# Late expert slots in pairs of one expert, 512 tokens wide, with tokens of twelve slots loaded ahead

## The chip, the core and the metric

The kernel runs on one core of a Trainium2 chip. A core has TensorE (PE), which multiplies matrices and writes into PSUM; VectorE (DVE) and ScalarE (ACT), which work elementwise; GpSimd (POOL), which here does some additions and issues the indirect DMAs; and SyncE (SP), whose queue issues the plain DMAs. Each engine takes its instructions in the order of the program and waits for the others by semaphores. In the profile a matmul has two rows: PEld is the load of the 128x128 stationary operand, PE the matmul itself.

The metric is the device time of one execution in microseconds, the median of several runs.

## The reference

A long convolution by Fourier transform is followed by a mixture of experts with one expert per token:

```
h_filt = (relu(pos_emb @ w1) @ w2) * exp(-0.01 * pos)
y      = irfft(rfft(x * v) * rfft(h_filt))[:S]         # along the sequence, for each channel
out    = x * y                                          # 4 x 11456 tokens of 128 channels
token is computed if  out @ w_skip > 0                  # about half of the 45824
e      = argmax(out @ w_gate),  g = softmax(out @ w_gate)[e]
out    = out + g * (relu(out @ moe_w1[e]) @ moe_w2[e])  # moe_w1[e] 128 x 1024, moe_w2[e] 1024 x 128
```

The other tokens keep `out`. There are eight experts.

## The kernel before

**Stages.** `first_phase` does the first of the transform's steps, `freq_phase` the products in the frequency domain (until about 850 us), `out_phase` the way back. `out_phase` works through 32 chunks (residues of the position modulo 32), each in three blocks, in a list of steps numbered 0 to 107. A step loads z and x for a block some blocks ahead (`load`, L993 and L982, with ZT = 5 buffers each), makes the product (L1004), multiplies by x, transposes, scores the tokens, chooses the expert and writes lists of the chosen tokens, and stores the rows to the output.

**Slots.** The experts' work is cut into 93 slots of up to 256 tokens of one expert (128 pairs of neighbours). `KNOWN = ((3, 4), (5, 5), ...)` says after how many chunks how many slots are fixed: a *table* (`table`, L544 on) counts the tokens of each expert so far and takes as many full slots as it says. The rest, partly filled ones among them, come from a last table after the last chunk. For each slot `reach`, `find` and `name` find where its tokens stand in the lists, one name for each step: POOL reads the token numbers (`name`, L645, tile `ids`). With them POOL loads the slot's tokens (`gather`, L679, two DMAs into one of XT = 7 tiles `xt`) and, when the slot is done, adds them back (`store`, L742, two DMAs from one of three tiles `o`).

**Early slots.** Slots 0 to 28 (`early_slots`) are done between the steps of `out_phase`: a generator that a step moves on 1.4 times, four times for each slot. Their first product runs on operands split in two float32r halves, three matmuls each (L736 to L738), their second in float32 (L801). A slot's tokens are loaded up to four slots ahead.

**Late slots.** Slots 29 to 92 (`late_slots`) follow one after another. In each iteration s, in the order of the program:

- one name, if any is left and s is even; the gather of slot s + FETCH (4);
- the tokens of slot s + 1 are transposed on PE (L725, into `mtp`) and split into high and low (`hl`: ACT L727, DVE L731); the first weight of slot s + 1 is split (`ws`: ACT L709, DVE L714);
- the first product of slot s in two halves of four 128-row blocks, 12 matmuls of 256 columns each, into one of two PSUM tiles `hp`; after each half ReLU on ACT and the low half on DVE (`hh`, L850 and L851); the second weight of slot s is split between them;
- after the first half, the result of slot s - 2 is transposed back (L832, into `mto`), gated and added (DVE L748) and stored;
- the second product of slot s - 1, 24 matmuls of 256 columns (L859 to L861) into `my`, and its copy to `yt` (ACT L866).

Both weights of all experts stay in SBUF; the expert of a slot is read from the table at run time. A loop for more than 93 slots stands at the end; with these inputs it makes no round, before as after.

The functions that the change touches, with what calls them:

Of the kernel before, what the change touches and what calls it, by code (L numbers as in the profile page):

```python
# [52 lines left out]
ZT = 5  # L53
XT = 7
FETCH = 4
NLATE = 64
NLAST = NEARLY + NLATE - NKNOWN
NTAB = 188

# [417 lines left out]
class Experts:  # L477
# [7 lines left out]
    def __init__(self, tc, i, out, lists, mc, wf):  # L485
# [48 lines left out]
        self.o, self.at = [mc.tile([128, 2, W], F32, name=f"o{k}") for k in range(3)], 0  # L534
# [9 lines left out]
    def table(self, counts, last, base, limit, pool, keep, ps):  # L544
# [20 lines left out]
        nc.vector.tensor_tensor(nt, ni, done, ALU.subtract)  # L565
        nc.vector.scalar_tensor_tensor(step, nt, float(-T2), step, ALU.mult, ALU.add)
# [25 lines left out]
        nc.vector.scalar_tensor_tensor(past[32:33, 0:limit], iota[32:33, 0:limit], float(T2), r, ALU.mult, ALU.add)  # L592
        row = pool.tile([1, NTAB], F32, name="trow", bufs=1)
        nc.vector.tensor_scalar(row[:, 0:limit], e, float(E - 1), float(F), ALU.min, ALU.mult)
        nc.vector.tensor_copy(self.tab[:, base:base + limit], row[:, 0:limit])
# [6 lines left out]
        spot = keep.tile([C, limit], F32, name=f"spot{base}")  # L602
        parts = keep.tile([LP + 1, limit, 2], F16, name=f"step{base}")
        si, sl = (pool.tile([C, NTAB], I32, name=f"ts{k}", bufs=1) for k in range(2))
        nc.vector.tensor_copy(spot, ps[0:C, 0:limit])
# [3 lines left out]
        nc.vector.memset(parts[LP:, :, 1], 1.0)  # L609
        nc.vector.tensor_tensor(parts[0:C, :, 0], si[:, 0:limit], sl[:, 0:limit], ALU.subtract)  # L610
        nc.vector.tensor_copy(parts[0:C, :, 1], sl[:, 0:limit])
        self.spots[base] = spot, parts
        if not last:

            dn = col("tdn")
            nc.vector.tensor_tensor(dn, cum, nt, ALU.subtract)
            nc.vector.tensor_scalar(dn, dn, -1.0, float(limit), ALU.mult, ALU.add)
            nc.vector.tensor_scalar(dn, dn, 0.0, None, ALU.max)
            nc.vector.tensor_tensor(dn, dn, nt, ALU.min)
            nc.vector.tensor_tensor(done, done, dn, ALU.add)  # L620
            return
# [64 lines left out]
    def space(self, pool):  # L686

        self.xts, self.held = [pool.tile([128, 2, W], F32, name=f"xt{k}") for k in range(XT)], 0
        for t in self.xts:
            self.nc.vector.memset(t, 0.0)  # L690
# [25 lines left out]
    def turn(self, xt, pool, tp):  # L716

        hl = self.orderhigh(xt, pool, tp)
        self.orderlow(hl, tp)
        return hl  # L720

    def orderhigh(self, xt, pool, tp):
        nc = self.nc
        for j in range(2):
            nc.tensor.transpose(tp[:, j * 128:(j + 1) * 128], xt[:, j, 0:D], self.ident)  # L725
        hl = pool.tile([128, 2, T], F32R, name="hl", bufs=2)
        nc.scalar.copy(hl[:, 0], tp[:, 0:T])  # L727
        return hl

    def orderlow(self, hl, tp):  # L730
        self.nc.vector.tensor_tensor(hl[:, 1], tp[:, 0:T], hl[:, 0].bitcast(F32), ALU.subtract)  # L731
# [18 lines left out]
    def early_slots(self, pool, psum, bank):  # L750
# [3 lines left out]
        def up(w, hl, u):  # L754
            hp = psum.tile([128, 2, T], F32, name="mh")
            for f in range(2):
                self.up(w, hl, hp[:, f], u * 2 + f)
            h = pool.tile([128, 2, T], F32, name="h", bufs=6)
            nc.scalar.activation(h, hp, AF.Relu)
            return h  # L760

        def turned(s):
            hp = psum.tile([128, 2, T], F32, name="mh")
            return self.turn(got[s][1], pool, hp[:, 0])
# [3 lines left out]

        def gather(s):
# [3 lines left out]
        for s in range(NEARLY):  # L773
            while s not in self.names:
                yield
            gather(s)
            if s not in hl:
                for _ in range(4):
                    yield
                    gather(s)  # L780
                w[s] = self.split(got[s][0], pool, 0, nc.vector)
                hl[s] = turned(s)
                yield
                yield
            tb, xt, ids, since = got.pop(s)
            wd[s] = pool.tile([128, F], F32, name="wd", bufs=1)
# [4 lines left out]
            if s + 1 in got:  # L791
                w[s + 1] = self.split_high(got[s + 1][0], pool, 0)
                hp = psum.tile([128, 2, T], F32, name="mh")[:, 0]
                hl[s + 1] = self.orderhigh(got[s + 1][1], pool, hp)
            yield
            if s + 1 in got:
                self.orderlow(hl[s + 1], hp)
# [13 lines left out]

    def late(self, s, pool):
        return self.gather(NEARLY + s, self.ids[:, NEARLY + s], pool, self.names[NEARLY + s])

    def late_slots(self, pool, queue):

        nc, tc = self.nc, self.tc
        with (
            tc.manual_schedule(),
            tc.tile_pool(name="mb", bufs=2) as mb,  # L820
            tc.tile_pool(name="mpt", bufs=1, space=PSUM) as mpt,
            tc.tile_pool(name="mph", bufs=2, space=PSUM) as mph,
            tc.tile_pool(name="mpy", bufs=2, space=PSUM) as mpy,
        ):
            def turned(st):
                return self.turn(st[1], pool, mpt.tile([128, T], F32, name="mtp"))

            def ends(yt):

                tp = mpt.tile([128, T], F32, name="mto")  # L830
                for j in range(2):
                    nc.tensor.transpose(tp[:, j * 128:(j + 1) * 128], yt[:, j * 128:(j + 1) * 128], self.ident)  # L832
                return tp

            def leave(st, tp):
                tb, xt, ids, since = st
                o = self.row()
                for j in range(2):
                    self.gated(o[:, j, 0:D], tp[:, j * 128:(j + 1) * 128], xt, j)
                    self.store(o[:, j], ids, j)  # L840

            def up(w, hl, u):
                hp = mph.tile([128, 4, T], F32, name="hp")
                for f in range(4):
                    self.up(w, hl, hp[:, f], u * 4 + f)
                return hp

            def relu(hp):
                h = mb.tile([128, 2, 4, T], F32R, name="hh", bufs=4)
# [4 lines left out]
            def down(w2, parts):  # L854
                y = mpy.tile([128, T], F32, name="my")
                for f in range(F // 128):
                    c = slice(f * D, (f + 1) * D)
                    h = parts[f // 4][:, :, f % 4]
# [3 lines left out]
                return y  # L862

            def drain(y):
                yt = mb.tile([128, T], F32, name="yt")
                nc.scalar.copy(yt, y)  # L866
                return yt

            st, w1, hl = ({s - NEARLY: v for s, v in d.items()} for d in self.ahead)
            for s in range(FETCH):  # L870
                if s not in st:
                    st[s] = self.late(s, pool)
            w2, hid, yt = {}, {}, {}
            for s in range(NLATE + 2):
                if queue and s % 2 == 0:
                    self.issue(queue.pop(0))
                if s + FETCH < NLATE:
                    st[s + FETCH] = self.late(s + FETCH, pool)
                if s + 1 < NLATE:
                    hl[s + 1] = turned(st[s + 1])  # L880
                if s + 1 < NLATE:
                    w1[s + 1] = self.split(st[s + 1][0], pool, 0, nc.vector)
                if s < NLATE:
                    hp = up(w1[s], hl[s], 0)
                if s >= 2:
                    leave(st.pop(s - 2), ends(yt.pop(s - 2)))
                if s < NLATE:
                    parts = [relu(hp)]
                    w2[s] = self.split(st[s][0], mb, 1, nc.vector)
                    hp = up(w1.pop(s), hl.pop(s), 1)  # L890
                    parts.append(relu(hp))
                    hid[s] = parts
                if 1 <= s <= NLATE:
                    yt[s - 1] = drain(down(w2.pop(s - 1), hid.pop(s - 1)))
            total = nc.values_load(self.total, min_val=0, max_val=NTAB - 1)
            with tc.For_i(NLAST, total, 1) as s:
                spot, parts = self.spots[NKNOWN]
# [3 lines left out]
                nc.vector.tensor_copy(step, parts[:, ds(s, 1)])  # L901
# [3 lines left out]
                ps = mpt.tile([128, T], F32, name="mto")[:, 0:2]  # L905
# [3 lines left out]
                x = turned(one)  # L909
                a = self.split(one[0], pool, 0, nc.gpsimd)  # L910
                b = self.split(one[0], mb, 1, nc.vector)
                parts = [relu(up(a, x, u)) for u in range(2)]
                leave(one, ends(drain(down(b, parts))))
# [24 lines left out]
def out_phase(tc, i, out, zd, ex, consts):  # L938
# [6 lines left out]
    with (  # L945
# [3 lines left out]
      with (  # L949
# [187 lines left out]
        for c, n in KNOWN:  # L1137
            checks[c - 1] = base, n
            base += n
        work = ex.early_slots(eb, eps, bank[2])  # L1140
# [6 lines left out]
        groups = [(ch, b, n) for ch, (b, n) in checks.items()] + [(NCH - 1, NKNOWN, NLAST)]  # L1147
# [39 lines left out]
        def routed(ch):  # L1187
            route(ch)
            last = ch == NCH - 1
            if last or ch in checks:  # L1190
                counts = ob.tile([E * NS, C], F16, name="now")
                nc.vector.tensor_copy(counts, ex.counts)
                span = (NKNOWN, NTAB) if last else checks[ch]
# [107 lines left out]
```

## Time and profile before

| | us |
|---|---|
| median of three runs | 1782.73 (1778.74 to 1784.9) |
| the profiled execution | 1785.03 |
| its span, first to last instruction | 1783.3 |
| mean granted clock of TensorE | 0.968 |
| busy: PE, DVE, POOL, ACT | 1625.3, 1320.7, 1054.8, 911.2 |

A row of instructions gives line, engine, operation, the tile written and the tiles read, the shape, the count after `x`, then busy time and mean ns of one, and the idle time of the engine before them with what ended it. A row of the timeline gives start and length in us first. PE counts as busy from a matmul's start to its modelled end, and matmuls overlap; how far apart they start tells what one costs.

### The profile page before, as it was taken

Reading aid. Unit: us, or ns where it says so; the run is one execution under the profiler, and the core shown is the slowest. Engines: PE = TensorE matmul, PEld = TensorE weight load, DVE = VectorE, ACT = ScalarE, POOL = GpSimd, SP = SyncE. Lnnn points to the kernel's source line nnn. Section 1 sums busy time; section 2 is a strip of 40 time slices with the busy share of each in tenths; the row PEclk is TensorE's granted clock in tenths of the full one; section 3 lists DMA queues with packets and bytes.
Section 4 is the critical chain, followed back from the end, with each engine's and each line's share of the span. In section 5 each row is a group of like instructions: output and inputs, shape, how many; then the busy total and the mean of one; then the engine's idle time right before and its main releaser. Section 6 shows DMA issues by size and latency. Waiting matters only on the chain. (4 is left out here: it accounts for less than half of the span.)

```text
span 1783.3 us, 30283 instructions
## 1 busy us (share of the span) xinstructions
PE 1625.3 (91%) x10053; PEld 1174.2 (66%) x10053; DVE 1320.7 (74%) x2476; ACT 911.2 (51%) x1670; POOL 1054.8 (59%) x767
## 2 busy tenths in 40 slices
PE   5987769999999799998678999999989999999996
PEld 3554445555556466554235677777778999999996
DVE  3433368777777899997387777778777888888885
ACT  4654435445554344343234555555545776666673
POOL 2111148667678699997004445325477887777785
PEclk8999889999999899999899999999998999999998
DMA  9999999999998699875998787788521111111110
GB/s 246 343 300 305 287 268 288 323 308 322 327 281 239 170 298 287 278 223 133 268 311 233 215 236 234 230 235 243 163 63 27 38 40 42 41 40 41 40 35 27
DMA packets 255137, 357.99 MB, mean 201 GB/s; under 512 B 24961, under 2 KB 189739, under 8 KB 254979
## 3 DMA queue, kind: packets, MB, share of 16 engines
q1 hardware_dynamic: 187692, 269.74, 50.8%
q10 hardware_dynamic: 47687, 47.71, 8.8%
q0 software_dynamic: 19600, 38.59, 7.9%
q8 instruction: 81, 1.33, 0.3%
q14 instruction: 77, 0.63, 0.1%
HBM read 212.91 MB, written 144.02 MB: 200 GB/s over the span
## 5 line engine op out<-in xcount | busy, mean ns | idle before, releaser
L411 POOL TENSOR_TENSOR y<-y,p 128x1024 f32<-128x1024 f32 x120 | 283.0, 2358 | 100.0 <-DVE y L409 95.3
L442 PE MATMUL zps<-y,c 128*128 128x512 f32 x720 | 339.4, 595 | 0.0
L742 POOL DMA_INDIRECT out<-o,ids x186 | 213.5, 1148 | 192.5 <-DVE o L748 144.1
L679 POOL DMA_INDIRECT xt<-out,ids x186 | 218.4, 1174 | 78.6 <-issue 29.9
L409 DVE TENSOR_TENSOR p<-xp,g 128x1024 f32<-128x1024 f32 x180 | 218.1, 1212 | 44.5 <-PE xp L415 29.2
L409 DVE TENSOR_TENSOR y<-xp,gc 128x1024 f32<-128x1024 f32 x180 | 218.3, 1213 | 20.0 <-PE xp L415 20.0
L714 DVE TENSOR_TENSOR ws<-wf,ws 128x1024 fp32r<-128x1024 f32 x157 | 191.6, 1221 | 51.3 <-ACT ws L709 45.1
L415 PEld LDWEIGHTS xp<-x,c 128*128 128x128 f32 x720 | 136.9, 191 | 110.7 <-issue 77.0
L415 PE MATMUL xp<-x,c 128*128 128x256 f32 x720 | 187.1, 382 | 15.0 <-DVE p L409 15.0
L443 ACT COPY z<-zps 128x512 f32<-128x512 f32 x180 | 104.0, 587 | 188.6 <-PE zps L442 186.5
L442 PEld LDWEIGHTS zps<-y,c 128*128 128x128 f32 x720 | 134.7, 191 | 99.5 <-issue 89.6
L396 ACT COPY gc<-t 64x384 f32<-64x384 f32 x240 | 113.7, 474 | 133.7 <-DVE y L409 92.0
L645 POOL DMA_INDIRECT ids<-lists,at x93 | 105.5, 1135 | 125.4 <-DMA zt<-zd 90.2
L709 ACT CAST ws<-wf 128x1024 fp32r x157 | 163.7, 1043 | 19.6 <-issue 13.9
L851 DVE SCALAR_TENSOR_TENSOR hh<-hp,hh 128x1024 fp32r<-128x1024 f32 x128 | 155.7, 1216 | 2.5 <-ACT hh L850 2.5
L736 PE MATMUL hp<-hl,ws 128*128 128x256 f32 x512 | 155.7, 304 | 1.2 <-DVE tb L668 0.6
L192 ACT COPY wf<-ps 120x512 f32<-120x512 f32 x192 | 110.5, 591 | 89.8 <-DMA x1d<-wf 40.9
L411 POOL TENSOR_TENSOR p<-p,p 128x1024 f32<-128x1024 f32 x60 | 149.5, 2492 | 0.0
L737 PE MATMUL hp<-hl,ws 128*128 128x256 f32 x512 | 145.4, 284 | 0.0
L738 PE MATMUL hp<-hl,ws 128*128 128x256 f32 x512 | 145.3, 284 | 0.0
L859 PE MATMUL my<-hh,ws 128*128 128x256 f32 x512 | 145.0, 283 | 0.0
L861 PE MATMUL my<-hh,ws 128*128 128x256 f32 x512 | 144.9, 283 | 0.0
(190 smaller groups left out, 3595.1 us busy)
## 6 DMA issues: line engine op xcount, KB each, us to landing
x<-x1d SPq DMA_DIRECT2D x60, 960.0 KB
x1d<-wf ACTq DMA_DIRECT2D x48, 960.0 KB
zd<-z SPq DMA_DIRECT2D x120, 384.0 KB
zt<-zd SPq DMA_DIRECT2D x96, 480.0 KB
out<-xm SPq DMA_DIRECT2D x96, 258.0 KB
ox<-xo SPq DMA_DIRECT2D x96, 256.0 KB
wf<-x SPq DMA_DIRECT2D x48, 480.0 KB
wf<-v SPq DMA_DIRECT2D x48, 480.0 KB
```

The costliest lines, as they stand in the source:

```text
L409: nc.vector.tensor_tensor(o, x[:, None].broadcast_to([128, 2, B, D]), v[:, :, None, :].broadcast_to([128, 2, B, D]), ALU.mult)
L411: add = lambda o, v: nc.gpsimd.tensor_tensor(o, o, v, ALU.add)
L415: nc.tensor.matmul(x[:, :, k], c2[:, k], x1[:, k, blk * B:(blk + 1) * B, :], start=True, stop=True)
L442: nc.tensor.matmul(zps, c3[:, a, :], y[:, blk, a], start=(a == 0), stop=(a == 1))
L679: ins = nc.gpsimd.indirect_dma_start(out=xt[:, j], out_offset=None, in_=self.rows[0:have], in_offset=bass.IndirectOffsetOnAxis(ap=ids[:, j ...
L709: nc.scalar.copy(w[:, 0], (self.w1f, self.w2f)[which][:, ds(self.where(nc.scalar, tb), F)])
L714: eng.tensor_tensor(w[:, 1], src[:, ds(self.where(eng, tb), F)], w[:, 0].bitcast(F32), ALU.subtract)
L736: nc.tensor.matmul(hp, w[:, 0, c], hl[:, 0], start=True, stop=False)
L737: nc.tensor.matmul(hp, w[:, 0, c], hl[:, 1], start=False, stop=False)
L738: nc.tensor.matmul(hp, w[:, 1, c], hl[:, 0], start=False, stop=True)
L742: ins = nc.gpsimd.indirect_dma_start(out=self.rows, out_offset=bass.IndirectOffsetOnAxis(ap=ids[:, j:j + 1], axis=0), in_=o, in_offset=Non ...
L851: nc.vector.scalar_tensor_tensor(h[:, 1], hp, 0.0, h[:, 0].bitcast(F32), ALU.max, ALU.subtract)
```

## The change

- **Pairs.** `KNOWN` has a third entry: 1 for single slots, 2 for pairs of slots of one expert. The first four tables give 29 singles, the early slots. The tables after 23 and 29 chunks give 12 and 10 pairs, the last table 20 singles: 22 pairs and 20 singles in place of 64 late slots. There is one table fewer.
- **Wide work.** A pair is one unit: four transposes into one `hl` of 512 columns, one split of each weight, a first product in four parts (two 128-row blocks each, six matmuls of 512 columns), and a second product in four parts of six.
- **Order.** Each part of the first product is followed on PE by a part of the previous unit's second product. The transposes back come after the first such part; the split of the first weight after the second, that of the second weight after the third. The copy to `yt` stands ahead of the fourth part's ReLU. Singles keep their order.
- **Ahead.** XT is 16; early slots gather up to twelve slots ahead, late units five units ahead (FETCH 5). Each unit issues one name.
- **Buffers.** ZT is 4, `o` has four tiles, `hh` six; `h` has five and lies with `wd` in another pool; the late pools wait for single tiles, not for whole pools.

The diff, cut to its core:

```diff
-KNOWN = ((3, 4), (5, 5), (8, 8), (13, 14), (22, 24), (26, 12), (29, 9))
-NKNOWN = sum(n for c, n in KNOWN)
-NEARLY = 29
+KNOWN = ((3, 4, 1), (5, 5, 1), (8, 8, 1), (13, 12, 1), (23, 12, 2), (29, 10, 2))
+NKNOWN = sum(n * u for c, n, u in KNOWN)
+NEARLY = sum(n for c, n, u in KNOWN if u == 1)
...
-ZT = 5
-XT = 7
-FETCH = 4
+ZT = 4
+XT = 16
+GATHERS = 12
+FETCH = 5
...
-        self.o, self.at = [mc.tile([128, 2, W], F32, name=f"o{k}") for k in range(3)], 0
+        self.o, self.at = [mc.tile([128, 2, W], F32, name=f"o{k}") for k in range(4)], 0
...
+    def turn_high(self, sts, pool, tp):
         nc = self.nc
+        for n, st in enumerate(sts):
+            for j in range(2):
+                nc.tensor.transpose(tp[:, n * T + j * 128:n * T + (j + 1) * 128], st[1][:, j, 0:D], self.ident)
+        hl = pool.tile([128, 2, 2 * T], F32R, name="hl", bufs=2)[:, :, 0:len(sts) * T]
+        nc.scalar.copy(hl[:, 0], tp[:, 0:len(sts) * T])
         return hl
...
         def gather(s):
-            for n in range(s, s + 4):
+            for n in range(s, min(s + GATHERS, XT - 1 + s)):
...
-            tc.tile_pool(name="mb", bufs=2) as mb,
+            tc.tile_pool(name="mb", bufs=2, reuse_waits="tile") as mb,
...
+            def up(w, hl, part):
+                n = hl.shape[2]
+                hp = mph.tile([128, 4 * T], F32, name="hp")
+                nf = 4 * T // n
+                for f in range(nf):
+                    self.up(w, hl, hp[:, f * n:(f + 1) * n], part * nf + f)
                 return hp
...
+            def down(w2, parts, n):
+                y = mpy.tile([128, 2 * T], F32, name="my")[:, 0:n]
+                nf = 4 * T // n
                 for f in range(F // 128):
...
+                    if k == nf - 1 and f < F // 128 - 1:
+                        yield
+                yt = mb.tile([128, 2 * T], F32, name="yt")[:, 0:n]
                 nc.scalar.copy(yt, y)
-                return yt
+                yield yt
...
+                parts = []
+                if u >= count:
+                    finish()
+                elif len(UNITS[u]) == 1:
+                    first()
+                    hp = up(w1[u], hl[u], 0)
+                    finish()
                     parts.append(relu(hp))
+                    second()
+                    parts.append(relu(up(w1[u], hl[u], 1)))
+                else:
+                    for k, rest in enumerate((finish, first, second, lambda: None)):
+                        hp = up(w1[u], hl[u], k)
+                        lower()
+                        parts.append(relu(hp))
+                        rest()
+                while u >= 1 and u - 1 < count and u - 1 not in yt:
+                    lower()
+                if u < count:
+                    before = down(w2[u], parts, hl[u].shape[2])
+                    del w1[u], hl[u]
```

Here `first` splits the first weight of unit u + 1, `second` the second weight of unit u, `finish` transposes, gates and stores unit u - 2, and `lower` issues the next part of the second product of unit u - 1.

More of the change, by code (lines that the diff above doesn't have):

```diff
@@ L810, in early_slots @@
             yield
-    def late(self, s, pool):
-        return self.gather(NEARLY + s, self.ids[:, NEARLY + s], pool, self.names[NEARLY + s])
+        yield from prepare(NEARLY)
     def late_slots(self, pool, queue):
@@ new lines, in leave @@
+            def leave(sts, yt):
+                tp = mpt.tile([128, 2 * T], F32, name="mto")
+                for j in range(2 * len(sts)):
+                    nc.tensor.transpose(tp[:, j * 128:(j + 1) * 128], yt[:, j * 128:(j + 1) * 128], self.ident)
+                for n, (tb, xt, ids, since) in enumerate(sts):
+                    o = self.row()
+                    for j in range(2):
+                        self.gated(o[:, j, 0:D], tp[:, n * T + j * 128:n * T + (j + 1) * 128], xt, j)
+                        self.store(o[:, j], ids, j)
```

208 lines of the change are left out of this document (107 added, 101 removed).

## The prediction

> **What bounds the kernel now.** I read the stretches first (columns: stretch, length, then busy time and instruction count of PE, PEld, DVE, ACT, POOL, granted clock, DMA share, GB/s), to see which stage the change touches and what fills it.
>
> ```profile
> 880.00:920.00 40.00, 28.81 (x260) 13.87 (x257) 29.87 (x116) 12.71 (x44) 0.00 (x0) 0.96 1.04 314
> 1000.00:1100.00 100.00, 98.25 (x904) 72.81 (x901) 75.78 (x282) 54.54 (x132) 44.45 (x41) 1.00 0.79 227
> 1330.00:1340.00 10.00, 6.17 (x43) 4.37 (x43) 4.36 (x16) 1.04 (x1) 7.87 (x8) 0.83 0.09 22
> 1500.00:1600.00 100.00, 94.49 (x784) 92.87 (x782) 83.50 (x120) 68.07 (x91) 79.56 (x68) 1.00 0.15 42
> 1700.00:1740.00 40.00, 40.00 (x339) 40.00 (x338) 36.23 (x53) 28.91 (x39) 32.07 (x27) 1.00 0.12 34
> ```
>
> The output stage with its early slots starts short of data (DMA share 1.04) and is full of PE from 1000 us on. The late slots are PE's too, but at 1500 to 1600 PE runs 784 instructions in 100 us against 339 in 40 us (848 in 100) near the end. To size that I took the tiles hp and yt (min/median/max ns, first and last start) and two drains of the undisturbed part:
>
> ```profile
> L736 PE MATMUL hp<-hl,ws x512: 278/283/552, 1353.3 to 1761.5; 128*128 128x256 f32 x171
> ```
> ```profile
> L866 ACT COPY yt<-my x64: 372/373/376, 1365.4 to 1768.8; 128x256 f32<-128x256 f32 x64
> ```
> ```profile
> 1421.16 0.37 ACT L866 COPY yt<-my 128x256 f32<-128x256 f32 x1 [1.52 <-PE my L861]
> ...
> 1427.35 0.37 ACT L866 COPY yt<-my 128x256 f32<-128x256 f32 x1 [1.53 <-PE my L861]
> ```
>
> An undisturbed slot takes 6.19 us; 64 of them are 396.2. From the first matmul to the last drain it took 1768.8 - 1353.3 = 415.5. So 19.3 us are no slot's work. Who makes PE wait, and what POOL does then (1360 to 1760, and 1360 to 1690 for the groups; the last row is the gathers at 1000 to 1300):
>
> ```profile
> PE mtp L725 <- DMA xt<-out,ids: 11.8, 17, 1.4
> ```
> ```profile
> L679 POOL DMA_INDIRECT xt<-out,ids x96 | 123.3, 1284 | 29.3 <-DMA out<-o,ids 14.4 <-issue 12.8 <-DMA ids<-lists,at 0.9
> L742 POOL DMA_INDIRECT out<-o,ids x96 | 109.3, 1139 | 29.3 <-issue 15.5 <-DMA xt<-out,ids 7.3 <-DVE tb L668 6.4
> ```
> ```profile
> L679 POOL DMA_INDIRECT xt<-out,ids x42 | 43.9, 1044 | 12.8 <-issue 6.7 <-PE mh L738 2.1 <-PE tp L1017 1.5
> ```
> ```profile
> 1532.92 1.04 POOL L645 DMA_INDIRECT ids<-lists,at  x1 [0.30 <-DMA out<-o,ids]
> ...
> 1546.22 1.04 POOL L645 DMA_INDIRECT ids<-lists,at  x1 [0.30 <-issue]
> ```
>
> POOL runs one after another with 0.30 us between: two slots need nine operations (a name, four gathers, four stores), 13.30 us from name to name, while PE needs 2 x 6.19 = 12.38. The late stage is **POOL's** while names are left and PE's afterwards. PE's 17 waits sum to 11.8 us of idle time; with refilling the array I put them at 16, and the other 3 to the half clock at the start and the last drain.
>
> **The change, part by part.** *Width.* A pair's 96 matmuls of 256 columns become 48 of 512, with the same eight transposes. What each costs, PE in the late stage and then the weight loads of the first phase, one for each 512-column fp32r matmul:
>
> ```profile
> 1420.90 0.38 PE L725 MATMUL mtp<-ident,xt 128*128 128x128 f32 x2
> 1421.04 0.36 PE L736 MATMUL hp<-hl,ws 128*128 128x256 f32 x1
> 1421.24 0.28 PE L737 MATMUL hp<-hl,ws 128*128 128x256 f32 x1
> ```
> ```profile
> 198.68 2.73 PEld L191 LDWEIGHTS ps<-ur,c1r 120*120 120x120 f32 x12 [0.25 <-issue]
> ```
> ```profile
> 202.42 2.38 PEld L191 LDWEIGHTS ps<-ur,c1r 120*120 120x120 f32 x11 [1.02 <-DVE ur L203]
> ...
> 206.76 0.18 PEld L191 LDWEIGHTS ps<-ur,c1r 120*120 120x120 f32 x1 [1.96 <-ACT ur L202]
> ```
>
> Two transposes with the first matmul behind them: 1421.24 - 1420.90 = 0.34. With 0.11 for a transpose (0.14 from the first of them to L736, less its early start) a 256-column matmul is 0.12. Check: 48 x 0.12 + 4 x 0.11 = 6.20, the period above. 512 columns: (2.73 - 0.18) / 11 = 0.232; the shorter burst gives (2.38 - 0.18) / 10 = 0.220, and no gain at all would be 0.240. A pair: 48 x 0.232 + 8 x 0.11 = 12.0 against 12.38. I take 0.232, the longer row: 22 pairs x 0.37 = **-8** (ends: 0 at 0.240, -21 at 0.220).
>
> [...]
>
> *ACT and DVE in a pair.* One split of each weight serves two slots; the ReLUs stay 128x1024 (1360 to 1760):
>
> ```profile
> L714 DVE TENSOR_TENSOR ws<-wf,ws 128x1024 fp32r<-128x1024 f32 x124 | 151.3, 1221 | 45.3 <-ACT ws L709 44.3 <-DVE at L640 0.6 <-issue 0.3
> L851 DVE SCALAR_TENSOR_TENSOR hh<-hp,hh 128x1024 fp32r<-128x1024 f32 x122 | 148.4, 1216 | 2.3 <-ACT hh L850 2.3
> ...
> L709 ACT CAST ws<-wf 128x1024 fp32r x125 | 130.3, 1042 | 14.2 <-issue 12.4 <-DVE tb L668 1.1 <-DVE hh L851 0.5
> L850 ACT ACTIVATE hh<-hp 128x1024 fp32r<-128x1024 f32 x123 | 126.0, 1025 | 9.2 <-PE hp L738 9.2
> ...
> L748 DVE SCALAR_TENSOR_TENSOR o<-mto,xt 128x128 f32<-128x128 f32 x120 | 36.5, 345 | 0.0
> ```
>
> DVE: 4 x 1.22 + 2 x 1.22 + 4 x 0.35 and under 1 for hl and tb, some 9.6 us; ACT: 4 x 1.03 + 2 x 1.04 and some 1.2 for hl and yt, 7.4. Both lie under PE's 12.0, so nothing is added or gained. The tight place is hp, two buffers: a part's bank is wanted again after one part of the first product and two of the second, 3 x 6 x 0.232 = 4.2 us, and its ReLU and subtraction take 2.3 with at most one split (1.2) ahead. The fourth part is worse: ACT has the copy of y ahead of it, which waits for the last of the second product. 1.4 + 0.6 (the 0.37 row twice as wide, less its fixed part) + 1.03 + 1.22 = 4.2 after the part's end, against 4.2 and two groups of four transposes (0.9). It fits by 0.9 us.
>
> *Tokens ahead.* POOL's operations for a pair stay nine, so at 13.30 against 12.0 it falls behind by 1.3 us a pair. What changes is how much it may. Before, the gather issued at slot s is wanted three slots on, 18.6 us; now it is issued five units ahead and wanted four units on, 48 us among pairs and 25 among singles. In program order 70 of 93 slots were named and slots up to 31 gathered when the late stage began; now 67 and 40. The second to the seventeenth unit gather for pairs and add 16 x 1.3 = 21 us of arrears on top of some 11 at the start. Before it was 14, from PE's 1353.3 to the first late name, the 71st:
>
> ```profile
> 1367.04 1.00 POOL L645 DMA_INDIRECT ids<-lists,at  x1 [0.30 <-issue]
> ```
>
> and two operations fewer stand ahead of it now. The last five pairs need seven operations (10.3 us) and give back 8. About 24 at the first single, where 25 are allowed: the waits just don't come back. I take **-16** for the waits and +1 for singles that still wait (ends: 0 and -17).
>
> Part of POOL's length is DVE's doing. An operation that starts under a weight split is longer (1.18 us, where the name above took 1.04):
>
> ```profile
> 1536.66 1.22 DVE L714 TENSOR_TENSOR ws<-wf,ws 128x1024 fp32r<-128x1024 f32 x1
> 1537.60 1.18 POOL L742 DMA_INDIRECT out<-o,ids  x1 [0.30 <-issue]
> ```
>
> [...]
>
> *The join.* The second late slot's transposes stand on PE ahead of the last early slot, and waited:
>
> ```profile
> 1333.06 1.01 POOL L679 DMA_INDIRECT xt<-out,ids  x1 [0.31 <-issue]
> ...
> 1335.60 0.33 PE L725 MATMUL mtp<-ident,xt 128*128 128x128 f32 x1 [2.75 <-DMA xt<-out,ids]
> ...
> 1337.01 0.47 PE L725 MATMUL mtp<-ident,xt 128*128 128x128 f32 x1 [1.08 <-DMA xt<-out,ids]
> ```
>
> 3.8 us, and the clock falls behind it (0.83 in that stretch; I put 2 us on it). In program order these tokens are now loaded 20 steps of four or five us earlier. The 20 last slots need two more rounds of places and sums than 17 did, +1. **-5** (ends: 0 and -6). Late next is the last table's own chain on DVE, which stays.
>
> *Loads of z and x.* Four buffers for five: each load starts up to a block later.
>
> ```profile
> PE y L1004 <- DMA zt<-zd: 18.4, 6, 13.5
> ```
>
> The 13.5 is the stage's first load; the other five waits are 4.9 us. From 1000 us on PE's own work covers a later load; before it there is no cover. **+2** (ends: 0 and +5, those waits once more). The table dropped and the larger ones beside it, o, h and wd in other pools, late pools that wait tile by tile (the first late matmul needs the last sums of places anyway), and gathers moved ahead of POOL's names and stores: 0, since PE works meanwhile and POOL is busy 44 of 100 us there. Uncovered, 24 gathers at 1.35 would be 32 us of POOL, spread over 100 us.
>
> Sum: -8 - 16 + 1 - 5 + 2 = -26. The profiled execution took 1785.0 (span 1783.3), 2.3 above the median of the three runs; 1785.0 - 26 = 1759, and against the median **1757**.
>
> **Rivals.**
>
> *POOL stays the limit.* Before, POOL had 23 names, 116 gathers and 128 stores to do from the first late name on (program order); now 26, 104 and 128, nine fewer at 13.30 / 9 = 1.48 us: -13 in place of the -28 for width, waits and join. With the +2, 1785 - 11 - 2.3 = 1772. For it: nothing of POOL's work in a pair shrinks. Against: the rate holds only if DVE blocks it as often.
>
> *The wide matmul is as short as the shorter burst.* 0.220 us: 13 us more than I take, 1744. Against: the longer burst, and its last load may be missing. [...]
>
> *Starved loads.* In program order 26 blocks go before the first early slot. If each loses 1 us for the missing buffer, +26 takes the gain back: 1783. For it: DMA share 1.04 there. Against: three blocks stay in flight.
>
> *Slower: the fourth part's ReLU.* If ACT or DVE reach it 2.4 us later than I count (a split that slips in front on both), the second part of the next pair waits 1.5 us for its bank, each pair 1.5: +33, 1790. It decides from 1.4 us a pair on; against it stand 2.4 us of free time on DVE and 4.6 on ACT in each pair.
>
> **How the numbers follow.** 0.60 for the forecast (1757, its own range 1748 to 1767), 0.18 POOL, 0.08 the short matmul, 0.08 starved loads, 0.06 slower. From 1743 to 1775 the first three lie inside, 0.86; a few of them miss by other terms. 0.3% (5.3 us) is about what can be told from no change here: faster 0.86, same 0.08, slower 0.06.
>
> **What would show it.** Wide matmuls 0.23 apart and drains 12.0 us apart in pairs; PE's waits for xt near 0 past 1360; no 3.8 us before the last early slot; POOL 10 to 30 us behind PE at the last pair, without a wait. Waits of PE for hp's buffer in pairs, a longer stretch before 1000 us, or waits for xt among the singles would make me wrong.

## The result

The changed kernel takes 1756.78 us (median of 4 runs, 1752.5 to 1761.34), the kernel before 1783.82 beside it (4 runs): ratio 0.9848, 95% interval 0.9806 to 0.989, 27 us less. The prediction was 1757. Its profiled execution took 1761.34, 23.7 less than the one of before, and the difference lies in three stretches:

| stretch, by rows of the profile | before | after | difference |
|---|---|---|---|
| output stage: first to last start of the products y | 435.5 | 441.4 | +5.9 |
| join: last product to the first late matmul | 63.0 | 60.1 | -2.9 |
| late stage: first late matmul to the last drain | 415.5 | 389.2 | -26.3 |

What lies ahead of the output stage differs by 0.4 us, and what follows the last drain takes 14.5 us in both. The stretches of after (columns as in the prediction) that answer to those of before:

```profile
880.00:920.00 40.00, 27.53 (x254) 13.51 (x250) 27.88 (x101) 13.21 (x46) 0.00 (x0) 0.96 1.03 281
1000.00:1100.00 100.00, 98.00 (x895) 72.55 (x894) 76.85 (x288) 53.53 (x129) 46.20 (x45) 1.00 0.85 233
1330.00:1340.00 10.00, 10.00 (x84) 9.08 (x85) 7.68 (x31) 3.71 (x6) 8.06 (x7) 0.83 0.12 28
1500.00:1600.00 100.00, 100.00 (x473) 82.75 (x472) 74.72 (x108) 58.74 (x68) 72.92 (x71) 1.00 0.15 41
1700.00:1740.00 40.00, 40.00 (x338) 40.00 (x338) 35.42 (x46) 28.54 (x38) 27.72 (x23) 1.00 0.10 30
```

At 1500 to 1600 PE is full, where it had 94.49 of 100 us. At 880 to 920, with the DMA engines as full as before, 281 GB/s flow where 314 did: here something was lost. The matmuls of the late stage, then three drains, of after, and the rows of both tiles, whose first and last starts (1355.9 and 1745.1) bound the late stage of the table:

```profile
1421.61 0.39 PE L761 MATMUL hp<-hl,ws 128*128 128x512 f32 x1
...
1424.11 0.39 PE L884 MATMUL my<-hh,ws 128*128 128x512 f32 x1
```
```profile
1400.88 0.59 ACT L888 COPY yt<-my 128x512 f32<-128x512 f32 x1 [2.12 <-PE my L884]
1412.70 0.59 ACT L888 COPY yt<-my 128x512 f32<-128x512 f32 x1 [2.12 <-PE my L884]
1424.54 0.59 ACT L888 COPY yt<-my 128x512 f32<-128x512 f32 x1 [2.12 <-PE my L884]
```
```profile
L761 PE MATMUL hp<-hl,ws x336: 278/389/765, 1355.9 to 1737.8; 128*128 128x512 f32 x88, 128*128 128x256 f32 x80
L888 ACT COPY yt<-my x42: 372/586/587, 1377.2 to 1745.1; 128x512 f32<-128x512 f32 x22, 128x256 f32<-128x256 f32 x20
```

Eleven steps from the first to the last of these matmuls: 2.50 / 11 = 0.227 us each, at a granted clock of 1.00. A pair takes 11.83 us, 0.55 less than two slots. PE's waits between 1360 and 1760 (total, times, longest), all of them, and POOL's two large groups between 1360 and 1690:

```profile
PE mto L895 <- ACT yt L888: 1.0, 2, 0.5
PE hp L761 <- DVE hh L871: 0.9, 2, 0.8
PE hp L761 <- DVE tb L692: 0.8, 1, 0.8
```
```profile
L767 POOL DMA_INDIRECT out<-o,ids x106 | 112.4, 1060 | 43.2 <-issue 14.3 <-DVE o L773 10.9 <-DMA out<-o,ids 6.4
L703 POOL DMA_INDIRECT xt<-out,ids x93 | 100.3, 1078 | 28.4 <-issue 23.2 <-DMA out<-o,ids 1.8 <-PE mtp L750 1.5
```

The 17 waits for tokens are gone. POOL's stores take 1060 ns (1139 before) and its gathers 1078 (1284 before), and POOL now waits for DVE's results, 10.9 us in all.

### The profile page after: what moved, and what is told of

The parts are those of the page before. It is cut to its first block, busy times and chain, and to the rows that moved or that the text cites. A ratio compares the mean times of both kernels' runs of the same rounds, so it can differ in the third digit from the quotient of the medians.

```text
span 1759.6 us, 27314 instructions
## 1 busy us (share of the span) xinstructions
PE 1615.1 (92%) x8980; PEld 1121.0 (64%) x8980; DVE 1269.8 (72%) x2404; ACT 862.7 (49%) x1582; POOL 1020.3 (58%) x767
## 5 line engine op out<-in xcount | busy, mean ns | idle before, releaser
L767 POOL DMA_INDIRECT out<-o,ids x186 | 201.6, 1084 | 178.0 <-DVE o L773 128.5
L703 POOL DMA_INDIRECT xt<-out,ids x186 | 199.1, 1070 | 93.1 <-issue 42.5
L870 ACT ACTIVATE hh<-hp 128x1024 fp32r<-128x1024 f32 x128 | 132.1, 1032 | 74.2 <-PE hp L763 74.2
L738 DVE TENSOR_TENSOR ws<-wf,ws 128x1024 fp32r<-128x1024 f32 x113 | 137.8, 1220 | 18.1 <-ACT ws L733 11.8
L204 PE MATMUL ps<-ur,c1r 120*120 120x512 f32 x300 | 113.3, 508 | 37.9 <-ACT ur L215 20.4
L1071 PE MATMUL y<-zt,c 120*64 120x512 f32 x384 | 108.4, 643 | 32.0 <-DMA zt<-zd 25.9
L833 PEld LDWEIGHTS bank<-wd,h 128*128 128x128 f32 x928 | 107.8, 191 | 30.9 <-issue 30.8
L761 PE MATMUL hp<-hl,ws 128*128 128x512 f32 (+1 forms) x336 | 122.2, 364 | 2.4 <-DVE hh L871 0.9
L733 ACT CAST ws<-wf 128x1024 fp32r x113 | 117.8, 1043 | 10.4 <-issue 5.1
```

What stands on the lines that cost most here:

```text
L703: ins = nc.gpsimd.indirect_dma_start(out=xt[:, j], out_offset=None, in_=self.rows[0:have], in_offset=bass.IndirectOffsetOnAxis(ap=ids[:, j ...
L733: nc.scalar.copy(w[:, 0], (self.w1f, self.w2f)[which][:, ds(self.where(nc.scalar, tb), F)])
L738: eng.tensor_tensor(w[:, 1], src[:, ds(self.where(eng, tb), F)], w[:, 0].bitcast(F32), ALU.subtract)
L761: nc.tensor.matmul(hp, w[:, 0, c], hl[:, 0], start=True, stop=False)
L767: ins = nc.gpsimd.indirect_dma_start(out=self.rows, out_offset=bass.IndirectOffsetOnAxis(ap=ids[:, j:j + 1], axis=0), in_=o, in_offset=Non ...
L870: nc.scalar.activation(h[:, 0], hp, AF.Relu)
```

## Experiments

All ratios are to the kernel before, run on the same chip beside each kernel.

**Width alone.** Each 512-column matmul of the first product done as two of 256 with the same weights; the second product likewise, into two tiles (not shown):

```diff
-                    self.up(w, hl, hp[:, f * n:(f + 1) * n], part * nf + f)
+                    for a in range(0, n, T):
+                        self.up(w, hl[:, :, a:a + T], hp[:, f * n + a:f * n + a + T], part * nf + f)
...
```

> The changed kernel with each matmul of 512 columns in a pair done as two of 256 columns with the same weights (the sum for y in two PSUM tiles, copied one after the other); pairs, shared splits and order stay. Theory (the gain of width is PE's alone, 0.227 us for 512 columns against twice 0.12): a pair takes 12.3 to 12.5 us instead of 11.83, +10 to +14 us in all. Rival (a matmul costs what its columns cost, and the shorter period comes from splits and waits): a pair stays at 11.8, 0 to 3 us.

1769.62 us, ratio 0.9934 (0.9913 to 0.9955). The drains of this kernel in its pairs:

```profile
1496.60 0.73 ACT L891 COPY yt<-my 128x256 f32<-128x256 f32 x2 [2.00 <-PE my L886]
1508.98 0.73 ACT L891 COPY yt<-my 128x256 f32<-128x256 f32 x2 [2.00 <-PE my L886]
1521.37 0.73 ACT L891 COPY yt<-my 128x256 f32<-128x256 f32 x2 [2.00 <-PE my L886]
```

12.38 us a pair, exactly two slots of before; the late stage is 11.6 us longer than in the changed kernel, the median 12.8. Width is worth 22 x 0.55 = 12 us and is PE's alone: splits shared by two slots give nothing while PE is full.

**Tokens ahead alone, in single slots.** The kernel before with 16 tiles for tokens, early gathers twelve slots and late ones ten slots ahead (`h` has five tiles in place of six, not shown):

```diff
-XT = 7
-FETCH = 4
+XT = 16
+FETCH = 10
...
-            for n in range(s, s + 4):
+            for n in range(s, s + 12):
```

> The kernel before with tokens ahead alone: 16 tiles for tokens (XT 16), early gathers up to twelve slots ahead, late ones ten slots ahead (FETCH 10); single slots, 256 columns and five buffers for z and x stay. Theory (what counts is how far POOL may fall behind, not how fast it is): POOL falls behind 0.9 us in each two slots and 33 us in all, 56 are allowed, so PE's waits for tokens go without any change in width: first matmul of the late slots to the last drain 400 instead of 415.5, the join 3 us shorter, 16 to 20 us faster in all, near 0.990 of before. Rival (the waits went because a pair halves the weight splits, so that POOL's operations got shorter): at 1.48 us an operation POOL stays the limit, the waits stay at 10 us or more, and it is at most 6 us faster.

1792.24 us, ratio 1.0054 (1.0033 to 1.0075): slower, by either theory a miss. Its waits between 1360 and 1760, PE's and then the first of DVE's:

```profile
PE hp L736 <- DVE hh L851: 10.0, 15, 1.0
PE hp L736 <- DVE tb L668: 5.5, 18, 0.6
```
```profile
DVE o L748 <- DMA out<-o,ids: 39.7, 43, 2.3
```

No wait for tokens is left, and yet the late stage takes 423.4 us. POOL is as far behind as ever; its stores are late now, one of the three result tiles `o` is not free, DVE stands in front of it for 39.7 us, and the subtraction behind it, which PE wants, is late. The wait had moved from the input of the slot to its output. The output stage also took 6.5 us longer, with DMA packets of 87 ns at 860 to 890 us where before had 74. What makes packets longer is dealt with below; where the buffers of this kernel lie is not on record.

**Room at both ends, still single slots.** The same with eight result tiles (and four buffers for z and x, placed at multiples of 256 bytes):

```diff
-        self.o, self.at = [mc.tile([128, 2, W], F32, name=f"o{k}") for k in range(3)], 0
+        self.o, self.at = [mc.tile([128, 2, W], F32, name=f"o{k}") for k in range(8)], 0
```

> The kernel before with tokens ahead (16 tiles, ten slots ahead) as in the run before, and eight tiles for results instead of three, four buffers for z and x, buffers at multiples of 256 bytes; single slots, 256 columns. Theory (in single slots POOL's arrears only moved from the tokens to the result tiles; room at both ends is enough, pairs are not needed for the waits): DVE no longer waits for a store to free its result tile (39.7 us in the run before), late stage 398 to 403 us instead of 415.5, the whole near 1763. Rival (POOL's rate is the limit in single slots whatever the room, and only the shorter operations of pairs lift it): the late stage stays above 408, the whole at 1770 or more.

1762.94 us, ratio 0.9882 (0.9859 to 0.9906). A stretch of it, then its matmuls and its drains:

```profile
1380.00:1690.00 310.00, 310.00 (x2610) 310.00 (x2610) 276.88 (x401) 225.07 (x302) 248.97 (x201) 1.00 0.15 39
```
```profile
L736 PE MATMUL hp<-hl,ws x512: 278/283/415, 1340.3 to 1732.0; 128*128 128x256 f32 x171
L866 ACT COPY yt<-my x64: 372/373/376, 1352.3 to 1739.3; 128x256 f32<-128x256 f32 x64
```

PE does not stand once in 310 us. The late stage is 1739.3 - 1340.3 = 399.0, 16.5 less than before, without a pair. POOL's operations are no shorter here (stores 1.25 us on average between 1360 and 1690, against 1.14 before). It simply falls behind: by the order of stores and results, a store starts 8 us after its result at first and up to 42 us after it later, and 19.6 us pass after the last drain in place of 14.5. So the theory holds: in single slots room at both ends is enough. The changed kernel with its buffers at multiples of 256 bytes too (1754.27 us, below) is 8.7 us faster than this one: no more than that is what pairs add to room at both ends.

**Pairs without the distance.** The changed kernel with 10 tiles, early gathers four slots and late ones two units ahead:

```diff
-XT = 16
-GATHERS = 12
-FETCH = 5
+XT = 10
+GATHERS = 4
+FETCH = 2
```

> The changed kernel with tokens no further ahead than before: 10 tiles for tokens, early gathers four ahead, late ones two units ahead (four slots among pairs). Theory (distance is needed in pairs too): nine POOL operations at 1.1 us and 0.3 between them are 12.5 us against PE's 11.83 in a pair, 0.7 us a pair on top of some 11 us at the start, and one unit, 12 us, is all that is allowed: PE waits again, 10 to 15 us in all. Rival (pairs alone cure it, since POOL's operations get shorter with half the splits): waits of 0 to 3 us.

1785.38 us, ratio 1.0007 (0.9988 to 1.0025), 29 us above the changed kernel. PE's largest wait between 1350 and 1760:

```profile
PE mtp L750 <- DMA xt<-out,ids: 22.2, 4, 17.8
```

The 17.8 is one wait at the join: the tokens of the second pair stand on POOL behind names and gathers that all come at once there. The other waits lie at the join (0.9) and at the first singles (3.5); among the 22 pairs there is none. Neither theory had this: pairs do cure the waits among themselves, as the rival said, and distance is needed all the same, at the join.

**A second operand on DVE.** Why does POOL keep up in pairs? The changed kernel with one more two-input operation in each pair:

```diff
+                        if k == 0:
+                            scrap = mb.tile([128, 1024], F32, name="scrap", bufs=1)
+                            nc.vector.tensor_tensor(scrap, self.w1f[:, 0:1024], self.w2f[:, 0:1024], ALU.subtract)
                         rest()
```

> The changed kernel with one more DVE operation with two SBUF inputs (128x1024, 1.22 us, result unused) in each pair, right ahead of the four operations that write the result tiles, as the split of the first weight stands in single slots. DVE then has 10.8 us of work in a pair of 11.83. Theory (what made POOL's operations long before was a split followed by the result operations: 1.65 us on average for the 50 that began so, 1.0 to 1.17 for all others): one or two POOL operations a pair get 0.5 us longer, POOL falls 0.5 to 1 us a pair behind and PE waits from the second half of the pairs on, +5 to +15 us. Rival (the length of a POOL operation has nothing to do with DVE): POOL's mean stays at 1.08 us and the time within 2 us, or moves by DVE's own lateness only, with waits for hh and none for xt.

1784.38 us, ratio 1.001 (0.9992 to 1.0029): +28 us, more than either theory had. Its waits between 1360 and 1760, PE's and then DVE's for result tiles; then a piece of its timeline, and one of after's:

```profile
PE hp L761 <- DVE hh L871: 20.4, 14, 1.8
```
```profile
DVE o L773 <- DMA out<-o,ids: 31.2, 34, 2.2
```
```profile
1509.63 1.21 DVE L738 TENSOR_TENSOR ws<-wf,ws 128x1024 fp32r<-128x1024 f32 x1
1509.83 1.88 POOL L703 DMA_INDIRECT xt<-out,ids  x1 [0.30 <-DMA ids<-lists,at]
1511.89 1.21 DVE L738 TENSOR_TENSOR ws<-wf,ws 128x1024 fp32r<-128x1024 f32 x1
1512.01 1.96 POOL L703 DMA_INDIRECT xt<-out,ids  x1 [0.30 <-issue]
```
```profile
1502.55 0.99 POOL L703 DMA_INDIRECT xt<-out,ids  x1 [0.30 <-issue]
1502.75 1.22 DVE L738 TENSOR_TENSOR ws<-wf,ws 128x1024 fp32r<-128x1024 f32 x1
1503.85 1.03 POOL L767 DMA_INDIRECT out<-o,ids  x1 [0.30 <-issue]
1505.18 1.00 POOL L767 DMA_INDIRECT out<-o,ids  x1 [0.31 <-issue]
1505.50 1.22 DVE L738 TENSOR_TENSOR ws<-wf,ws 128x1024 fp32r<-128x1024 f32 x1
```

Here an operation that POOL began just behind the start of a split lasted 1.9 us; one that began ahead of a split, or at its very end, 1.0. Grouped by how long after the start of the last such DVE operation (a split, or the added one) each POOL operation began, as count and mean length:

| began after | before, 1360 to 1690 | after, 1376 to 1600 | this run, 1376 to 1600 |
|---|---|---|---|
| 0 to 0.2 us | 5, 2.00 us | 0 | 27, 1.98 us |
| 0.2 to 0.4 | 20, 1.76 | 0 | 9, 1.82 |
| 0.4 to 0.6 | 9, 1.69 | 3, 1.57 | 5, 1.66 |
| 0.6 to 0.8 | 16, 1.42 | 0 | 0 |
| 0.8 to 1.0 | 50, 1.16 | 6, 1.12 | 9, 1.20 |
| later | 119, 1.02 | 156, 1.01 | 92, 1.01 |

So a POOL operation that began in a split's first microsecond ended 0.85 to 0.92 us after the split, however early it began (all 100 of before, all 9 of after). Of those that began later than that, but within a microsecond ahead of the next split, the 94 of before lasted 1.00 to 1.04 us and the 38 of after 0.98 to 1.00. DVE's being busy was not enough: the 50 operations of before that began under the subtraction for `hh` alone, which is as long as a split but has one of its inputs in PSUM, lasted 1.00 to 1.04 us, and the 73 of after 0.98 to 1.04. In the changed kernel 9 of 165 operations begin in a split's first microsecond, before 100 of 219, in this run 50 of 142. Most of this run's long operations began under the two splits that after has too: 34 did so, of 1.88 us on average, where after has 38 of 1.09. So the added operation also moved the others against each other. The distance from a result to its store stays at 3.5 to 6.7 us through most of after's pairs; here it grows from 2 to 25 us, until the four result tiles are used up. Then the pairs take 13.85 us in place of 11.83. Until then, for seven pairs with the added operation in them, they keep 11.8, so DVE's own work is not what costs. The theory's cause is shown, and its size was off because I had counted only tokens, not result tiles, as the room that POOL may use.

**The output stage.** Three runs. First the buffers for z and x alone, in the kernel before:

```diff
-ZT = 5
+ZT = 4
```

> The kernel before with the one edit ZT 5 to 4: four buffers for z and x in place of five, everything else as it was. Theory (the missing buffer is what the changed kernel lost in the output stage): the products of the fourth to the twelfth block fall back by 5 to 7 us and stay back, the last product starts near 1296 instead of 1289.9, and since POOL's operations of the late slots start with the stage before them, the whole is 5 to 7 us slower. Rival (the early gathers twelve slots ahead, or o and h in other pools, cost the stage its 6 us): 0 to 2 us slower, as my sum had it.

1782.0 us, ratio 0.9998 (0.9978 to 1.0017). Its products, and those of before, of after, and of the two runs that follow:

```profile
L1004 PE MATMUL y<-zt,c x384: 592/630/1117, 853.9 to 1290.8; 120*64 120x512 f32 x192
```
```profile
L1004 PE MATMUL y<-zt,c x384: 592/643/1116, 854.8 to 1290.3; 120*64 120x512 f32 x192
```
```profile
L1071 PE MATMUL y<-zt,c x384: 592/615/1116, 854.4 to 1295.8; 120*64 120x512 f32 x192
```
```profile
L1072 PE MATMUL y<-zt,c x384: 592/614/1116, 851.0 to 1287.1; 120*64 120x512 f32 x192
```
```profile
L1005 PE MATMUL y<-zt,c x384: 592/643/1116, 849.0 to 1295.1; 120*64 120x512 f32 x192
```

436.9, 435.5, 441.4, 436.1 and 446.1 us from the first to the last start. The missing buffer costs 1.4 us at most, not 6: the theory of this run fell. (Three profiles of the changed output stage, after's and those of the runs with narrow matmuls and with the second operand, give 440.8 to 443.4, so 1.4 is no more than their scatter.) What else differed was where the buffers lie. In the compiled programs they begin at a multiple of 256 bytes in the kernel before, and 64 bytes past one in the changed kernel, since tiles ahead of them have other sizes (the addresses stand in the expectations below; a trace shows none). So 192 unused bytes in the changed kernel, and, with 16 for 48, 64 in the kernel before:

```diff
         ex.space(eb)
+        keep.tile([128, 48], F32, name="pad")
```

> The changed kernel with 192 unused bytes put ahead of the output stage's tiles, so that each buffer for z and x begins at a multiple of 256 bytes in SBUF, as in the kernel before (there the address is 256 modulo 512, in the changed kernel 64). Theory (the 6 us of the output stage are longer DMA packets, 77 against 67 ns for 1024 bytes in 858 to 895 us, and they come from where the tiles lie): packets near 67 ns again, last product 4 to 6 us earlier, 0.997 of the changed kernel. Rival (it is the fourth buffer, or the longer early loading of tokens): packets and last product as in the changed kernel.

> The kernel before with 64 unused bytes ahead of the output stage's tiles, so that the buffers for z and x begin 64 bytes past a multiple of 256. Theory (place in SBUF): 1024-byte packets of 74 to 80 ns instead of 67 in 858 to 895 us, last product 4 to 6 us later, and the whole as much slower, 1.003. Rival (buffers or gathers): no difference.

1754.27 us, ratio 0.9837 (0.9818 to 0.9856), for the changed kernel with the buffers moved, and 1789.52, ratio 1.0038 (1.0021 to 1.0055), for the kernel before with its buffers shifted. What the DMA engines did at 860 to 890 us, where they are full, in before, after, the moved and the shifted (packets, MB, share of 16 engines):

```profile
q1 hardware_dynamic: 6713, 8.12, 104.0%
```
```profile
q1 hardware_dynamic: 5978, 7.26, 104.1%
```
```profile
q1 hardware_dynamic: 6491, 7.91, 103.6%
```
```profile
q1 hardware_dynamic: 5894, 7.15, 104.1%
```

Share x 16 engines x 30 us over packets gives 74, 84, 77 and 85 ns a packet: the place of the buffers makes the packets 9 to 14% longer (the 1024-byte packets alone: 67, 77, 68 and 78 ns), and that costs the stage 5.3 us in the changed kernel and 10.6 in the kernel before, of which 4.8 are left at the last product, as its products began earlier. The theory holds. The unused bytes shift every tile of the stage that lies behind them, those that rows are stored from too, so which tiles count is not separated. Between the changed kernel and the moved one the whole times' intervals overlap, so that gain stands on the stage, not on the total; the moved one has the lowest median of all that was run.

**The fourth part's ReLU.** The changed kernel with one, and in a second kernel two, more copies on ACT ahead of it:

```diff
+                        if k == 3:
+                            for _ in range(1):
+                                scrap = mb.tile([128, 1024], F32, name="scrap", bufs=1)
+                                nc.scalar.copy(scrap, self.w1f[:, 0:1024])
                         parts.append(relu(hp))
```

> The changed kernel with one more copy of 128x1024 on ACT (1.04 us, result unused) ahead of the fourth part's ReLU in each pair. Theory (my count of 0.9 us between the fourth part's ReLU with its subtraction and the moment PE wants the bank back): the copy eats the 0.9 and 0.1 us a pair is left over, 0 to +4 us in all. Rival (ACT is late there already, and what it is late by is hidden in the pair's 11.83 us): +15 us or more.

> The changed kernel with two such copies, 2.08 us, ahead of the fourth part's ReLU in each pair. Theory (0.9 us of room): 1.2 us a pair are not covered, 22 pairs, +20 to +30 us, and PE waits for hh. Rival (there is more room than I counted, so that the slower case of my prediction was further off): under +8 us.

> The same kernel with two copies of 128x1024 on ACT (2.08 us) ahead of the fourth part's ReLU in each pair, once more, since the kernel before took 1952 us beside it where it takes 1783 elsewhere, with gaps of up to 9 us in which all of PE, ACT and DVE stood. Theory (0.9 us of room): 1.2 us a pair are not covered, +20 to +30 us against the changed kernel, ratio to the kernel before 0.996 to 1.002, PE waits for hh. Rival (more room than I counted): under +8 us, ratio under 0.990.

1957.95 us for one copy, 1963.55 and 1960.35 for two. Beside these runs the kernel before itself took 1950 us, with gaps of up to 9 us in which PE, ACT and DVE all stood; their cause is not known to me, and the totals (ratios 1.0093, 1.0127 and 1.008) can't be held against those of the changed kernel. Between the gaps the pairs are regular. Drains with one copy, and with two (the last run):

```profile
1516.98 0.59 ACT L888 COPY yt<-my 128x512 f32<-128x512 f32 x1 [2.12 <-issue]
1529.29 0.59 ACT L888 COPY yt<-my 128x512 f32<-128x512 f32 x1 [1.60 <-PE my L884]
```
```profile
1528.97 0.59 ACT L888 COPY yt<-my 128x512 f32<-128x512 f32 x1 [2.12 <-PE my L884]
1542.31 0.59 ACT L888 COPY yt<-my 128x512 f32<-128x512 f32 x1 [2.12 <-PE my L884]
```

12.31 and 13.34 us a pair: 0.48 and 1.51 above 11.83 for copies of 1.04 and 2.08. The room is 0.56 and 0.57 us, the same from both. I had counted 0.9. One copy would thus cost 22 x 0.48 = 11 us (between my two theories), two 33.

**The join.** The single-slot kernel with room at both ends, and the changed kernel's tables:

```diff
-KNOWN = ((3, 4), (5, 5), (8, 8), (13, 14), (22, 24), (26, 12), (29, 9))
+KNOWN = ((3, 4), (5, 5), (8, 8), (13, 12), (23, 24), (29, 20))
```

> The single-slot kernel with room at both ends (tokens ten slots ahead, eight result tiles, buffers at multiples of 256 bytes) with the tables of the changed kernel: after 3, 5, 8, 13, 23 and 29 chunks 4, 5, 8, 12, 24 and 20 slots, 20 left for the last table instead of 17. Theory (tokens ahead were worth 5 us or more at the join, and the changed kernel gave 2 to 4 of them back for the later tables and two more rounds of places): from the last product to the first late matmul 60 to 62 us instead of 57.9, +2 to +4 us in all. Rival (the join differs by how many slots are loaded there or by the granted clock alone): 57 to 59 us, no difference.

1956.43 us, ratio 1.0053, beside the same 1950 us of the kernel before. The gaps lie in its join too (85 us), so this run decides nothing. On that chip the changed kernel with the copies on ACT, whose tables are the same, has a join of 85.4 to 85.7 us. That the two agree fits the tables as the cause, but the same gaps lie in both, and the question stays open.

## Why the prediction was right, and where it was not

The two large terms, width and PE's waits for tokens, were right in kind. That the total fits to a microsecond is luck: four of its terms were off and cancelled, and the four runs themselves lie up to 9 us apart.

| step | predicted | measured |
|---|---|---|
| width | -8 | -12 (11.83 us a pair; +12.8 when undone) |
| waits for tokens | -16 | -16.5 (the single-slot kernel with room; -14.2 is what the late stage of after leaves beside the width) |
| waits of the singles | +1 | 0 |
| join | -5 | -2.9 (-1.3 in the profiles of two other kernels with this join) |
| loads of z and x | +2 | +1.4 at most |
| o, h, wd in other pools | 0 | +4.5, what is left of 5.9, by the place of the buffers (5.3 when they were moved) |

- **Width** was mis-sized: I took 0.232 us for a 512-column matmul from the longer of two bursts, and it is 0.227, midway between that and the shorter burst's 0.220.
- **The waits** were sized rightly and explained wrongly in part. I let POOL fall 1.3 us a pair behind, to some 24 us at the first single, with distance as the cure. In after POOL keeps step with the pairs and even waits for a result from 1571 us on:

```profile
1571.64 1.02 POOL L767 DMA_INDIRECT out<-o,ids  x1 [2.22 <-DVE o L773]
```

  From there to the last pair its stores start 0.3 to 6.5 us after their results, so "POOL 10 to 30 us behind PE at the last pair" is refuted. That part of POOL's length is DVE's doing was a remark in the prediction, without a term of its own, and it was what counted: in pairs, with half the splits, POOL's operations took 1.02 us on average (after, 1376 to 1600) against 1.20 (before, 1360 to 1690), and the run with the added operation shows how much hangs on it. In the table of POOL's operations the longest group takes 1.0 us more than the shortest. Distance alone, which I took for the cure, made the late stage of single slots 7.9 us longer: I had counted the tiles that POOL fills and not those that it empties.
- **Loads**: the step as written (one buffer less) was right at no more than 1.4 for 2. The step that failed is the one behind it, in which the other pools were put at nothing: they moved the buffers of z and x off their multiple of 256 bytes.
- **The join**: in the two single-slot kernels with tokens ahead it is 55.7 and 57.3 us against 63.0, so the tokens are worth the 5 and more that I gave them. The changed kernel gives back some 3 to 6, where I had 1 for two more rounds of places. The granted clock is part of it: it is half for 9.8 us of the join before, for 1.2 and 3.4 in those two kernels, for 4.6 in after, and for 7.6 and 8.4 in the two kernels whose join is 61.7 us. PE's waits on DVE for places and for the expert are 6.6 us in after and 5.2 before. That the later tables and rounds are the cause of the rest is argued only, and the late pools that wait tile by tile were not tried alone.
- **ACT and DVE in a pair**: no waits, as said, but by 0.56 us of room and not 0.9.
- Of the **rivals**, POOL as the limit was closest: one more two-input operation of 1.2 us brings it about and takes the whole gain. The slower case stayed away by less than I thought.

Sum of the measured terms against before: -12 - 16.5 - 2.9 + 5.9 = -25.5; the profiled executions differ by 23.7. The 2 us between are in the late stage. After its first matmul the granted clock is half for 5.6 us in after and for 3.4 in the single-slot kernel with room, which is 1.1 us of work, and PE waits 0.8 us more, as much as one wait where the singles begin.

## What to carry to other kernels

When one engine issues both the loads and the stores of a pipeline and falls behind, count the free tiles at both ends: here more room at one end alone moved the wait to the other (39.7 us of DVE's waits for result tiles), and either room at both ends (16.5 us off the late stage) or shorter operations of the issuing engine (1.02 us for 1.20, no wait for tokens among the pairs even at two units ahead) removed it. When a change alters the sizes of tiles, look where the DMA buffers behind them come to lie, in any stage that fills the DMA engines: 64 bytes past a multiple of 256 cost the output stage 5.3 and 10.6 us here. And take a total that fits as a reason to check its terms one by one.

## What the runs showed of the hardware

- An indirect DMA of POOL that began in the first microsecond of a split on DVE, an operation of 1.22 us with two SBUF inputs, ended 0.85 to 0.92 us after that operation (100 such in before, 9 in after) and took up to 2.04 us, where those that began later took 1.01 to 1.02 on average. Those that began within a microsecond ahead of a split took 1.00 to 1.04 us (94 in before) and 0.98 to 1.00 (38 in after), and those under a DVE operation of the same length with one input in PSUM 1.00 to 1.04 (50 in before) and 0.98 to 1.04 (73 in after). So the relative timing of the two engines counted: in the changed kernel 9 of 165 POOL operations began in a split's first microsecond, with a third such operation in each pair 50 of 142, and 34 of that run's long ones began under the same two splits.
- With the buffers 64 bytes past a multiple of 256 and the DMA engines full (share 104%, 860 to 890 us), packets took 84 ns on average in the changed kernel and 85 in the kernel before with its buffers shifted, where at a multiple of 256 they took 77 in the changed kernel with its buffers moved and 74 in the kernel before.
- At a granted clock of 1.00, 512-column fp32r matmuls started 0.227 us apart (after, 1421.61 to 1424.11), 256-column ones 0.12 (before, 1361.16 to 1365.11).
